# Attention and two gated layers on one core: the 1e-9 of the softmax on GpSimd, weight conversions once a pair and in two parts, and two transfers in another place

## The chip, the cores and the metric

The kernel runs on one core of one Trainium2 chip. Times are device microseconds of one execution. A core has TensorE (PE, matmuls and transposes), VectorE (DVE), ScalarE (ACT), GpSimd (POOL) and SyncE (SP), whose queue issues nearly all of this kernel's transfers. Each engine takes its instructions in a fixed order, and waits for semaphores of the others.

## What is computed

Causal attention with a decay, in float32, for 4 batches of 8 heads, 576 positions and 64 columns; its output, laid out as 2304 tokens of 512, runs through two gated layers.

```python
scores = np.matmul(q, k.transpose(0, 1, 3, 2)) / sqrt(D)
cum = np.cumsum(np.log(np.clip(f, 0.0001, 1.0)), axis=-1)
decay = cum[:, :, :, None] - cum[:, :, None, :]
scores = np.where(causal, -1e9, scores + decay)
attn = np.exp(scores - scores.max(-1, keepdims=True))
attn = attn / (attn.sum(-1, keepdims=True) + 1e-09)
x = np.matmul(attn, v)          # then (B * S, H * D)
x = (sigmoid(x @ w_gate) * (x @ w_val)) @ w_out
h = x @ w_in
return (h * np.clip(h + 3, 0, 6) / 6) @ w_out2
```

## The kernel before

**Pairs and steps.** Two heads make a pair; there are 16 pairs, and each is worked in four steps of query rows: first step s = 1 (the first 256 rows), second s = 2 and third s = 3 (128 rows each), fourth s = 4 (the 64 left over, both heads together). The loop near the end of the kernel counts steps by `t`, so pair i has t = 4i to 4i+3. Pairs 7 to 15 run their steps backwards. In step t TensorE multiplies the masks and the scores of unit t into PSUM (`st`); VectorE reads them, adds the decay and takes the least (`expo`, L500); ScalarE takes the exponential and sums it (L508). `norm` (L540 on) works one step later: VectorE adds 1e-9 to the sums (L543), takes the reciprocal (L544), and GpSimd multiplies the rows `e` by it (L546). Three steps after its scores a unit is turned by TensorE (`flip`, `tt<-ident,e`), and ScalarE copies it to `etA` or `etB`. So TensorE turns the fourth step of the pair before in the third step of this pair, behind that step's masks. In the third step also stand the products with v of the pair before (`values`, `pv`), whose result ScalarE and VectorE split in two (L645, L646) and SP stores in `x_d` (L650).

**Two banks.** The scores of a step take two of three PSUM tiles, so the masks of a step wait until VectorE has read the first tile of the step before. VectorE's reads thereby set TensorE's pace.

**Weights.** The weights of the gated layers come as float64 bits. A conversion (`single`, `convert`) takes a tile `raw` of 128x1024 words: VectorE shifts (L107) and merges (L108), ScalarE scales (L111), VectorE merges again (L114), and a high part (L64 on GpSimd, later L62 on ScalarE) and a low part (L65 on GpSimd) are made. `Converter.run` counts up a share per step and converts a tile when it comes to 1: before t = 24 it adds 0.38 (`CE`), then 0.65 (`CA`), near the end 0.12 (`CS`). That puts the first conversions at t = 6, 9, 11, 14, 17, 19 and 22. From t = 23 on TensorE also has a group of 12 products of the first gated layer in most steps (`fill.one`, `pg` and `pv` on `big`), which need the converted weights and `x_d` of the first four pairs (`big<-x_d`, L205).

**Order.** TensorE's order is written out by hand. For the other engines a scheduler chooses, among what `tc.issue_after` and `tc.high_priority` leave free. Pairs 7 on load q and k in blocks (`load_blocks`, 8 transfers of 72 KB a pair) and turn them with VectorE. The sums of logarithms, times -8, which these pairs need, are made in a tile `eight` of the pool that also holds the rows `e`, and stored from it (`cum_d<-eight`) at t = 2.

Of the kernel before, what the change touches and what calls it, by code (L numbers as in the profile page):

```python
# [7 lines left out]
F32 = mybir.dt.float32  # L8
# [12 lines left out]
def attn_moe_kernel(  # L21
# [18 lines left out]
    P = 128  # L40
# [62 lines left out]

    def single(a_, b_, raw, e_exp):
        low, high = raw[:, :, 0], raw[:, :, 1]
        with tc.issue_after(pace["dve"].ins) if pace["dve"] is not None else ExitStack():
            nc.vector.tensor_scalar(low, low, 29, None, ALU.logical_shift_right)  # L107
        nc.vector.scalar_tensor_tensor(low, high, -(2**31), low, ALU.bitwise_and, ALU.bitwise_or)  # L108
        e = high.bitcast(F32)
        if e_exp is nc.scalar:  # L110
            nc.scalar.activation(e, e, AF.Copy, scale=2.0**-112)  # L111
        else:
            e_exp.tensor_scalar(e, e, 2.0**-112, 1.0, ALU.mult, ALU.mult)
        nc.vector.scalar_tensor_tensor(low, high, 3, low, ALU.logical_shift_left, ALU.bitwise_or)  # L114
        return low.bitcast(F32).rearrange("p (a b) -> p a b", a=a_)

    def convert(dst_hi, dst_lo, raw, e_exp, e_hi, e_lo):
        a_, b_ = dst_hi.shape[1:]
        split_sbuf(dst_hi, dst_lo, single(a_, b_, raw, e_exp), e_hi, e_lo)

# [8 lines left out]
    class Half:  # L129
# [10 lines left out]
        def __call__(self, engs):  # L140
            self.load()
            t, ks = self.t, self.ks
            if not self.shape:
                a_, b_ = self.src.shape[1], self.src.shape[2] // 2
                t.append(single(a_, b_, self.raw, engs[0]))
# [3 lines left out]
            convert(t[0][:, 0, ks], t[0][:, 1, ks], self.raw, *engs)  # L149
            if ks.start > 0:  # L150
                t.append(True)

    class Converter:


        def __init__(self):
            self.jobs, self.due, self.ahead = [], 0.0, 0

# [15 lines left out]

        def run(self, n, engs):
            self.due += n
            if self.due >= 1.0:
                drain()
            while self.due >= 1.0 and self.jobs:
                self.due -= 1.0  # L180
                self.jobs.pop(0)(engs)
            for job in self.jobs[: self.ahead]:
                if isinstance(job, Half):
                    job.load()
            if not self.jobs:
                self.due = 0.0
# [14 lines left out]
    def load_x(src, c, kc):  # L201
        t0, T = chunks[c]
        x = xr[ring["x"] % len(xr)][:, :, :T]
        ring["x"] += 1
        nc.sync.dma_start(  # L205
            x.bitcast(F32), src[:, kc * P : (kc + 1) * P, t0 : t0 + T].rearrange("a p t -> p a t")
        )
        return x
# [80 lines left out]
    def cumulate():  # L289
# [12 lines left out]
        nc.sync.dma_start(cum_d[0], cum)  # L302
        return cum, pick

# [16 lines left out]
    class Pair:  # L321
# [17 lines left out]
        def load(self):  # L339

            new = lambda nm: nat.tile([P, NKT, 2, D], F32, tag="nat", name=nm)
            if self.blocks:
                self.qn, self.kn = (self.load_blocks(new(nm), src) for nm, src in (("qn", q), ("kn", k)))
                return
            self.qn = load_nat(new("qn"), q, self.b, self.hp, ())
            self.kn = load_nat(new("kn"), k, self.b, self.hp, ((0, k), (TAIL, q)))
# [193 lines left out]
        def norm(self, s):  # L540
            m, n = self.m[s], len(self.es[s])
            with behind(reads[-1]), tc.high_priority():
                nc.vector.tensor_scalar(m[:, 8 : 8 + n], m[:, 4 : 4 + n], 1.0e-9, None, ALU.add)  # L543
                pace["dve"] = nc.vector.reciprocal(m[:, 12 : 12 + n], m[:, 8 : 8 + n])  # L544
# [103 lines left out]
        def store(self):  # L648
            rows, cols = (slice(i * n, i * n + n) for i, n in ((self.hp, P), (self.b, S)))
            nc.sync.dma_start(x_d[:, rows, cols].rearrange("a p t -> p a t"), self.x.bitcast(F32))  # L650

# [590 lines left out]

    KD, KT, RT = 4, 7, 0

    CA, C0, CB, CC = 0.65, 4, (1.8, 1.0, 1.5, 1.7, 2.0), 1.0

    CE, CS = 0.38, 0.12

# [22 lines left out]
    warm_up(WU[0])  # L1271
    cum, pick = cumulate()
    pairs[0].load()
# [11 lines left out]
    def scores(t):  # L1285
# [5 lines left out]
        if i == 0 and nxt:  # L1291
            if p.i:
                nxt.load()
            nxt.load_decay()
            nxt.load_v()
        p.scores(s)
# [148 lines left out]
```

## Time and profile before

| | us |
|---|---|
| median of three runs | 1005.12 (1002.36 to 1005.62) |
| the profiled execution | 1003.57 |
| its span, first to last instruction | 1001.8 |
| TensorE busy | 986.5 |
| VectorE, ScalarE, GpSimd busy | 530.9, 476.9, 290.5 |

The page's busy shares are means over stages that differ: the attention takes the first 275 us or so, the two gated layers the rest. What bounds a stage is read from the busy times in stretches, from the waits, and from the instructions in order of time.

### The profile page before, as it was taken

The numbers are of one execution on the slowest core, as the hardware profiler recorded it, in microseconds if no ns is written. First come the engines' busy times: TensorE is split into PE (matmuls) and PEld (weight loads), VectorE is DVE, ScalarE is ACT, GpSimd is POOL, SyncE is SP. The second block draws the span as 40 slices with busy tenths as digits, with TensorE's granted clock in tenths as the row PEclk, the third lists the DMA queues.
The fourth block names the chain that finished last, engine by engine and source line by source line (L and its number), as shares of the span: only waits on it lengthen the run. The fifth ranks groups of instructions, "written<-read, shape, count | busy, mean of one in ns | idle before, by whom it ended". The sixth has DMA issues, their size and how long they took to land.

```text
span 1001.8 us, 16150 instructions
## 1 busy us (share of the span) xinstructions
PE 986.5 (98%) x5733; PEld 810.4 (81%) x5733; DVE 530.9 (53%) x1220; ACT 476.9 (48%) x1094; POOL 290.5 (29%) x360
## 2 busy tenths in 40 slices
PE   8889999999999999999999999999999999999998
PEld 4556766667688889988888888899899898998987
DVE  6777856645347543737777574553534443333322
ACT  6787677667634432424434343453444443433322
POOL 3675655545323220302334131111111111111110
PEclk9999999999999999999999999999999999999999
DMA  7999796744324352566977578654686845753211
GB/s 184 294 250 226 198 244 156 185 143 145 119 79 154 117 166 82 175 210 264 331 258 252 179 270 318 245 198 166 237 330 206 293 147 193 294 209 148 81 66 64
DMA packets 141072, 197.30 MB, mean 197 GB/s; under 512 B 84192, under 2 KB 93408, under 8 KB 136896
## 3 DMA queue, kind: packets, MB, share of 16 engines
q1 hardware_dynamic: 140944, 196.20, 59.9%
q8 instruction: 45, 0.74, 0.3%
q14 instruction: 35, 0.29, 0.1%
q10 hardware_dynamic: 48, 0.07, 0.0%
HBM read 142.88 MB, written 53.36 MB: 196 GB/s over the span
## 4 chain that ended last, share of the span: by engine, by line
PE 91%; DVE 3%; ACT 2%; DMA 2%; issue 1%; POOL 0%; SPq 0%; DVEq 0%; ACTq 0%; POOLq 0%
PE po L216 34%; PE pv L216 18%; PE u L216 17%; PE pg L216 15%; PE st L216 4%; PE tt L220 3%; DVE e L500 1%; DMA kn<-in_k_dram 1%; ACT e L508 1%; DMA cum_d<-eight 1%; DMA x_d<-x 0%; DVE raw L108 0%; ACT raw L111 0%; ACT etB L580 0%; PE o L216 0%
## 5 line engine op out<-in xcount | busy, mean ns | idle before, releaser
L216 PE MATMUL po<-w,big 128*128 128x512 f32 x864 | 200.5, 390 | 0.0
L216 PEld LDWEIGHTS po<-w,big 128*128 128x128 f32 x864 | 161.8, 188 | 32.8
L216 PE MATMUL pg<-big,wg 128*128 128x512 f32 (+1 forms) x720 | 161.9, 371 | 0.0
L216 PE MATMUL pv<-big,wv 128*128 128x512 f32 (+1 forms) x720 | 161.4, 371 | 0.0
L216 PE MATMUL po<-big,wo 128*128 128x512 f32 (+1 forms) x720 | 160.9, 371 | 0.2 <-DVE big L65 0.2
L216 PEld LDWEIGHTS pg<-big,wg 128*128 128x128 f32 x720 | 125.8, 189 | 27.2 <-issue 4.0
L216 PEld LDWEIGHTS pv<-big,wv 128*128 128x128 f32 x720 | 125.6, 189 | 26.8 <-issue 4.5
L216 PEld LDWEIGHTS po<-big,wo 128*128 128x128 f32 x720 | 125.6, 189 | 25.7 <-issue 2.2
L1160 DVE TENSOR_TENSOR h<-h,u 128x384 f32<-128x384 f32 x69 | 38.2, 554 | 154.0 <-PE u L216 154.0
L546 POOL TENSOR_SCALAR e<-e,m 128x256 f32<-128x256 f32 (+4 forms) x144 | 86.8, 617 | 48.8 <-DVE m L544 32.1
L508 ACT ACTIVATE e<-e,m 128x256 f32<-128x256 f32 (+4 forms) x144 | 83.6, 584 | 31.6 <-DVE m L500 20.3
L216 PE MATMUL u<-h,big 128*128 128x384 f32 x504 | 90.2, 336 | 0.4 <-DVE h L1160 0.4
L216 PE MATMUL u<-h,h 128*128 128x384 f32 x504 | 90.1, 336 | 0.0
L216 PEld LDWEIGHTS u<-h,big 128*128 128x128 f32 x504 | 88.3, 188 | 1.8 <-DVE h L1160 0.8
L216 PEld LDWEIGHTS u<-h,h 128*128 128x128 f32 x504 | 88.4, 188 | 1.0
L1109 POOL TENSOR_TENSOR big<-tail,big 128x384 fp32r<-128x384 f32 x30 | 30.5, 1018 | 196.5 <-PE u L216 115.5
L1157 ACT COPY h<-u 128x384 f32<-128x384 f32 x69 | 32.8, 475 | 111.5 <-PE u L216 111.5
L500 DVE CUSTOM_DVE_ANT_0 e<-st,dc 128x384 f32<-128x384 f32 (+3 forms) x110 | 53.5, 520 | 47.9 <-PE st L216 30.3
L872 DVE SCALAR_TENSOR_TENSOR sg<-sg,pv 128x512 f32<-128x512 f32 (+1 forms) x48 | 29.7, 618 | 92.3 <-PE pv L216 59.7
L111 ACT ACTIVATE raw<-raw 128x512 f32<-128x512 f32 x68 | 45.6, 682 | 67.1 <-DVE raw L108 64.5
L62 ACT CAST big<-sg 128x512 fp32r<-128x512 f32 (+1 forms) x60 | 34.8, 580 | 60.6 <-DVE sg L872 54.6
L114 DVE SCALAR_TENSOR_TENSOR raw<-raw 128x512 int32<-128x512 int32 x68 | 52.5, 782 | 19.4 <-ACT raw L111 18.9
(141 smaller groups left out, 1202.8 us busy)
## 6 DMA issues: line engine op xcount, KB each, us to landing
h<-xc_d SPq DMA_DIRECT2D x21, 768.0 KB, 7.2
big<-x_d SPq DMA_DIRECT2D x28, 512.0 KB, 5.8
raw<-in_moe_w_out_dram SPq DMA_DIRECT2D x28, 512.0 KB, 3.7
h<-wt_d SPq DMA_DIRECT2D x12, 1024.0 KB, 7.4
big<-wt_d SPq DMA_DIRECT2D x12, 1024.0 KB, 7.6
x_d<-x SPq DMA_DIRECT2D x16, 576.0 KB, 3.9
h<-wb_d SPq DMA_DIRECT2D x12, 768.0 KB, 4.6
big<-wb_d SPq DMA_DIRECT2D x12, 768.0 KB, 5.2
```

The costliest lines, as they stand in the source:

```text
L62: nc.scalar.copy(hi, src)
L111: nc.scalar.activation(e, e, AF.Copy, scale=2.0**-112)
L114: nc.vector.scalar_tensor_tensor(low, high, 3, low, ALU.logical_shift_left, ALU.bitwise_or)
L216: i = nc.tensor.matmul(*a, **k)
L220: i = nc.tensor.transpose(*a)
L500: i = nc.vector.tensor_tensor_reduce(out=e, in0=st, in1=d, op0=ALU.add, op1=ALU.min, scale=self.by, scalar=init, accum_out=m[:, a : a + 1],)
L508: nc.scalar.activation(e, e, AF.Exp, bias=m[:, a : a + 1], scale=-1.0, accum_out=m[:, 4 + b : 5 + b])
L546: pace["pool"] = nc.gpsimd.tensor_scalar(e, e, m[:, 12 + j : 13 + j], 1.0, ALU.mult, ALU.mult)
L872: pace["dve"] = nc.vector.scalar_tensor_tensor(sg, sg, 1.0, pv, ALU.add, ALU.mult)
L1109: (nc.vector if f else nc.gpsimd).tensor_tensor(lo, sg, hi.bitcast(F32), ALU.subtract)
L1157: nc.scalar.copy({0: u1, 2: u2, 3: p5}[s], o)
L1160: tt(c, c, o, ALU.add)
```

## The change

Five things are changed.

1. `norm`: the 1e-9 is added on GpSimd, with high priority, and only the reciprocal stays on VectorE behind the last read. 64 small instructions change engine.
2. `single` is cut in two. `begin_single` holds L107, L108 and L111; `end_single` the second merge (now L118), with the high and low part behind it. While `conv.parts` holds (t up to 22), the end is put off to the `conv.run` of the next step, and stands behind that step's last read of scores.
3. The shares `CA` and `CE` give way to a list of steps `CW`: one conversion at t = 6, 10, 14, 18 and 22 (in the third step of a pair, beside `values`), and then at 23, 24, 26 to 30.
4. `KD` goes from 4 to 5: the copy of k of pair 4 is on VectorE and not ScalarE, one half of that pair's `values` is in another PSUM pool, and the high parts are on GpSimd until t = 20 and not 16.
5. Transfers: `eight` is put in the tile `fl` of `cumulate` and not in one of the pool of `e`; pair 7's loads of q, and pair 6's of v, stand behind the store of pair 3's x, and pair 7's loads of k behind the load of that x for the first gated layer.

```diff
-    def single(a_, b_, raw, e_exp):
+    def begin_single(raw, e_exp):
         low, high = raw[:, :, 0], raw[:, :, 1]
...
-        nc.vector.scalar_tensor_tensor(low, high, 3, low, ALU.logical_shift_left, ALU.bitwise_or)
+
+    def end_single(a_, raw):
+        low, high = raw[:, :, 0], raw[:, :, 1]
+        with tc.issue_after(pace["dve"].ins) if conv.parts else ExitStack():
+            nc.vector.scalar_tensor_tensor(low, high, 3, low, ALU.logical_shift_left, ALU.bitwise_or)
         return low.bitcast(F32).rearrange("p (a b) -> p a b", a=a_)
...
         def __call__(self, engs):
             self.load()
+            begin_single(self.raw, engs[0])
+            if conv.parts:
+                conv.rest.append(lambda: self.end(engs))
+            else:
+                self.end(engs)
...
         def run(self, n, engs):
+            while self.rest:
+                self.rest.pop(0)()
             self.due += n
...
-                self.qn, self.kn = (self.load_blocks(new(nm), src) for nm, src in (("qn", q), ("kn", k)))
+                first = self.i == KT
+                with behind(pairs[NP - 1].stored if first else None):
+                    self.qn = self.load_blocks(new("qn"), q)
+                with behind(pace["x"] if first else None):
+                    self.kn = self.load_blocks(new("kn"), k)
                 return
...
             m, n = self.m[s], len(self.es[s])
+            with tc.high_priority():
+                nc.gpsimd.tensor_scalar(m[:, 8 : 8 + n], m[:, 4 : 4 + n], 1.0e-9, 1.0, ALU.add, ALU.mult)
             with behind(reads[-1]), tc.high_priority():
-                nc.vector.tensor_scalar(m[:, 8 : 8 + n], m[:, 4 : 4 + n], 1.0e-9, None, ALU.add)
                 pace["dve"] = nc.vector.reciprocal(m[:, 12 : 12 + n], m[:, 8 : 8 + n])
...
-    KD, KT, RT = 4, 7, 0
-
-    CA, C0, CB, CC = 0.65, 4, (1.8, 1.0, 1.5, 1.7, 2.0), 1.0
-
-    CE, CS = 0.38, 0.12
+    KD, KT, RT = 5, 7, 0
+
+    C0, CB, CS = 4, (1.8, 1.0, 1.5, 1.7, 2.0), 0.12
+
+    CW = (6, 10, 14, 18, 22, 23, 24, 26, 27, 28, 29, 30)
...
-            nxt.load_v()
+            with behind(pairs[NP - 1].stored if p.i == NP + 1 else None):
+                nxt.load_v()
...
-            eight = ep.tile([P, S], F32, tag="e", name="eight")[: B * H]
             nc.vector.tensor_scalar(eight, cum, -8.0, 1.0, ALU.mult, ALU.mult)
...
+        conv.parts = t <= CW[4]
         if t >= C0:
-            conv.run(CS if len(conv.jobs) <= 2 * NSA - 6 * NGA else CE if t < NQ * (KT - 1) else CA, EA if t < NQ * KD else EF)
+            conv.run(CS if len(conv.jobs) <= 2 * NSA - 6 * NGA else float(t in CW), EA if t < NQ * KD else EF)
```

TensorE's order is the same before and after, instruction for instruction. Three places where the others' order differs:

GpSimd, from the multiplication of the unit t = 10 (128x512) to that of t = 11 (128x576), before. `wv` is the weight that is converted there, `dt` the masked decay of the next pair:

```order
L546 TENSOR_SCALAR e<-e,m 128x512 x2
L386 AFFINE_SELECT dt<-dc 64x576 x2
L64 TENSOR_SCALAR wv_818<-raw 128x512
L546 TENSOR_SCALAR e<-e,m 128x576
L65 TENSOR_TENSOR wv_818<-raw,wv_818 128x512
```

The same stretch now (`wg` is the weight); those up to the units t = 7, 15 and 19 read alike:

```order
L560 TENSOR_SCALAR e<-e,m 128x512 x2
L399 AFFINE_SELECT dt<-dc 64x576 x2
L64 TENSOR_SCALAR wg_601<-raw 128x512
L556 TENSOR_SCALAR m<-m 128x1
L65 TENSOR_TENSOR wg_601<-raw,wg_601 128x512
L556 TENSOR_SCALAR m<-m 128x4
L560 TENSOR_SCALAR e<-e,m 128x576
```

Two additions have come in, and the low part of the weight (L65) stands ahead of the multiplication 128x576, not behind it.

VectorE in the third and fourth step of pair 1 (t = 6 and 7), before. `raw` is the tile being converted, `x` the split result, and the ISA rows are the reads of scores:

```order
L107 TENSOR_SCALAR raw<-raw 128x512
L646 TENSOR_TENSOR x<-pv,x 128x256
L108 SCALAR_TENSOR_TENSOR raw<-raw 128x512
L114 SCALAR_TENSOR_TENSOR raw<-raw 128x512
L646 TENSOR_TENSOR x<-pv,x 128x320
L500 ISA e,m<-st,dt 128x288
L500 ISA m 128x1
L500 ISA e,m<-st,dt,m 128x288
```

And now:

```order
L107 TENSOR_SCALAR raw<-raw 128x512
L660 TENSOR_TENSOR x<-pv,x 128x256
L108 SCALAR_TENSOR_TENSOR raw<-raw 128x512
L660 TENSOR_TENSOR x<-pv,x 128x320
L513 ISA e,m<-st,dt 128x288
L513 ISA m 128x1
L513 ISA e,m<-st,dt,m 128x288
L513 ISA m 128x1
L558 RECIPROCAL m<-m 128x2
L118 SCALAR_TENSOR_TENSOR raw<-raw 128x512
```

The second merge has moved behind both reads and the reciprocal, and the addition L543 is gone.

SP around the loads of pair 7's blocks (`32x18x32`) and the store of pair 3's x, before. The first row is the store of pair 2's x, the store in the last but two rows that of pair 3's:

```order
L650 DMA x_d<-x 128x2x576
L352 DMA qn<-in_q_dram 32x18x32 x2
L101 DMA raw<-in_moe_w_val_dram 128x2x512
L352 DMA qn<-in_q_dram 32x18x32 x2
L205 DMA big<-x_d 128x2x512
L352 DMA kn<-in_k_dram 32x18x32 x4
L365 DMA dc<-cum_d_89 128x1152
L311 DMA vn_151<-in_v_dram 128x4x64 x2
L315 DMA vn_151<-in_v_dram 64x2x64
L650 DMA x_d<-x 128x2x576
L101 DMA raw<-in_moe_w_val_dram 128x2x512
L352 DMA qn<-in_q_dram 32x18x32 x4
```

And now, again from the store of pair 2's x; the second store is that of pair 3's:

```order
L664 DMA x_d<-x 128x2x576
L214 DMA big<-x_d 128x2x512
L101 DMA raw<-in_moe_w_gate_dram 128x2x512
L378 DMA dc<-cum_d_89 128x1152
L664 DMA x_d<-x 128x2x576
L320 DMA vn_151<-in_v_dram 128x4x64 x2
L324 DMA vn_151<-in_v_dram 64x2x64
L365 DMA qn<-in_q_dram 32x18x32 x2
L214 DMA big<-x_d 128x2x512
L365 DMA qn<-in_q_dram 32x18x32 x2
L365 DMA kn<-in_k_dram 32x18x32 x4
```

Pair 7's eight loads now stand behind the store of pair 3's x, and its loads of k also behind the load `big` of that x.

## Rows read from the trace of the kernel before

**Rows 1.** Busy times in two stretches, one of each stage
```profile
core 0: us, PE busy (x) PEld busy (x) DVE busy (x) ACT busy (x) POOL busy (x), PEclk, DMA share, GB/s
50.00:75.00 25.00, 21.82 (x226) 13.27 (x226) 19.91 (x75) 21.65 (x67) 18.95 (x27) 1.00 0.94 251
...
300.00:325.00 25.00, 25.00 (x112) 20.67 (x112) 17.83 (x27) 11.75 (x19) 8.01 (x6) 1.00 0.50 152
```

**Rows 2.** TensorE's waits: us in total, times, longest us
```profile
PE st L216 <- DVE m L500: 3.9, 8, 2.1
PE st L216 <- ACT raw L111: 2.5, 2, 1.4
PE tt L220 <- POOL e L546: 1.4, 3, 0.6
```

**Rows 3.** TensorE in order of time: start, us, engine, line, operation, count [idle before]
```profile
32.02 0.51 PE L216 MATMUL st<-masks,identb 128*128 128x384 bf16 x2 [2.06 <-DVE m L500]
...
44.46 0.50 PE L216 MATMUL st<-masks,identb 128*128 128x384 bf16 x2
...
51.41 0.52 PE L220 MATMUL tt<-ident,e 64*128 64x64 f32 x10 [0.54 <-POOL e L546]
...
58.19 0.50 PE L216 MATMUL st<-masks,identb 128*128 128x384 bf16 x2 [0.70 <-DVE m L500]
...
63.88 0.53 PE L220 MATMUL tt<-ident,e 64*128 64x64 f32 x10
...
70.24 0.50 PE L216 MATMUL st<-masks,identb 128*128 128x384 bf16 x2 [0.20 <-DVE m L500]
...
82.98 2.99 PE L216 MATMUL pg<-big,wg 128*128 128x512 f32 x12
85.81 0.50 PE L216 MATMUL st<-masks,identb 128*128 128x384 bf16 x2
```

**Rows 4.** Busy times and granted clock in the 4 us behind the longest wait
```profile
32.00:36.00 4.00, 3.98 (x30) 2.67 (x32) 2.87 (x15) 2.40 (x7) 3.21 (x4) 0.57 1.11 239
```

**Rows 5.** VectorE in order of time, in third and fourth steps of pairs
```profile
27.46 0.69 DVE L500 CUSTOM_DVE_ANT_0 e<-st,dc 128x512 f32<-128x512 f32 x1 [1.30 <-DMA cum_d<-eight]
...
30.49 0.69 DVE L114 SCALAR_TENSOR_TENSOR raw<-raw 128x512 int32<-128x512 int32 x1 [0.73 <-ACT raw L111]
...
58.28 0.52 DVE L500 CUSTOM_DVE_ANT_0 e<-st,dt,m 128x288 f32<-128x288 f32 x1
...
71.32 0.17 DVE L544 RECIPROCAL m<-m 128x2 f32<-128x2 f32 x1
```

**Rows 6.** GpSimd in order of time, in the first and second steps of three pairs
```profile
49.97 0.67 POOL L64 TENSOR_SCALAR wv<-raw 128x512 fp32r<-128x512 f32 x1
50.60 0.75 POOL L546 TENSOR_SCALAR e<-e,m 128x576 f32<-128x576 f32 x1
51.32 1.30 POOL L65 TENSOR_TENSOR wv<-raw,wv 128x512 fp32r<-128x512 f32 x1
...
60.26 1.37 POOL L546 TENSOR_SCALAR e<-e,m 128x512 f32<-128x512 f32 x2 [0.78 <-ACT etB L580]
61.58 1.40 POOL L386 TENSOR_SCALAR_AFFINE_SELECT dt<-dc 64x576 f32<-64x576 f32 x2
...
71.66 1.81 POOL L546 TENSOR_SCALAR e<-e,m 128x512 f32<-128x512 f32 x2 [1.32 <-DVE m L544]
73.43 1.91 POOL L386 TENSOR_SCALAR_AFFINE_SELECT dt<-dc 64x576 f32<-64x576 f32 x2
```

**Rows 7.** Groups of GpSimd by form, first 275 us: busy us, mean ns | idle before
```profile
L546 POOL TENSOR_SCALAR e<-e,m 128x128 f32<-128x128 f32 x32 | 12.4, 388 | 21.3 <-DVE m L544 14.8 <-PE tt L220 4.5 <-ACT e L508 2.0
...
L546 POOL TENSOR_SCALAR e<-e,m 128x576 f32<-128x576 f32 x16 | 12.2, 761 | 1.2 <-ACT e L508 0.6 <-DVE m L544 0.3
```

**Rows 8.** DMA issues from 20 to 110 us: count, KB each, median us to landing
```profile
x_d<-x SPq DMA_DIRECT2D x6, 576.0 KB, 4.9
...
qn<-in_q_dram SPq DMA_DIRECT2D x16, 72.0 KB, 5.1
```

**Rows 9.** SP's queue in order of time: start, us, and what it issued
```profile
64.68 3.47 SPq L352 DMA_DIRECT2D kn<-in_k_dram  x4
```

More of the change, by code (lines that the diff above doesn't have):

```diff
@@ L113, in single @@
             e_exp.tensor_scalar(e, e, 2.0**-112, 1.0, ALU.mult, ALU.mult)
-        nc.vector.scalar_tensor_tensor(low, high, 3, low, ALU.logical_shift_left, ALU.bitwise_or)
+    def end_single(a_, raw):
+        low, high = raw[:, :, 0], raw[:, :, 1]
+        with tc.issue_after(pace["dve"].ins) if conv.parts else ExitStack():
+            nc.vector.scalar_tensor_tensor(low, high, 3, low, ALU.logical_shift_left, ALU.bitwise_or)
         return low.bitcast(F32).rearrange("p (a b) -> p a b", a=a_)
-    def convert(dst_hi, dst_lo, raw, e_exp, e_hi, e_lo):
-        a_, b_ = dst_hi.shape[1:]
-        split_sbuf(dst_hi, dst_lo, single(a_, b_, raw, e_exp), e_hi, e_lo)
     pace = {"dve": None, "pool": None}
@@ L141, in __call__, with end @@
             self.load()
+            begin_single(self.raw, engs[0])
[3 more added lines that the diff above has]
+                self.end(engs)
+        def end(self, engs):
             t, ks = self.t, self.ks
+            w = end_single(ks.stop - ks.start if ks else self.src.shape[1], self.raw)
             if not self.shape:
-                a_, b_ = self.src.shape[1], self.src.shape[2] // 2
-                t.append(single(a_, b_, self.raw, engs[0]))
+                t.append(w)
                 return
@@ L148, in __call__ @@
                 t.append(self.pool.tile(self.shape, F32R, tag=self.tag, name=self.nm))
-            convert(t[0][:, 0, ks], t[0][:, 1, ks], self.raw, *engs)
+            split_sbuf(t[0][:, 0, ks], t[0][:, 1, ks], w, *engs[1:])
             if ks.start > 0:
@@ L156, in __init__ @@
         def __init__(self):
-            self.jobs, self.due, self.ahead = [], 0.0, 0
+            self.jobs, self.due, self.ahead, self.rest, self.parts = [], 0.0, 0, [], False
         def cols(self, pool, tag, w, c0, nm):
@@ L204, in load_x @@
         ring["x"] += 1
-        nc.sync.dma_start(
+        pace["x"] = nc.sync.dma_start(
             x.bitcast(F32), src[:, kc * P : (kc + 1) * P, t0 : t0 + T].rearrange("a p t -> p a t")
@@ L302, in cumulate @@
         nc.sync.dma_start(cum_d[0], cum)
-        return cum, pick
+        return cum, pick, fl
     def behind(i):
@@ L649, in store @@
             rows, cols = (slice(i * n, i * n + n) for i, n in ((self.hp, P), (self.b, S)))
-            nc.sync.dma_start(x_d[:, rows, cols].rearrange("a p t -> p a t"), self.x.bitcast(F32))
+            self.stored = nc.sync.dma_start(x_d[:, rows, cols].rearrange("a p t -> p a t"), self.x.bitcast(F32))
     def mm3(o, wh, wl, xh, xl, first, last, free=False):
@@ L1271, in attn_moe_kernel @@
     warm_up(WU[0])
-    cum, pick = cumulate()
+    cum, pick, eight = cumulate()
     pairs[0].load()
```

## The prediction

> **What bounds the kernel now.** I read the busy times in stretches first: where the two gated layers run, TensorE is busy 25.00 of 25 us, and in the attention's early pairs 21.82 [rows 1]. TensorE's order and work are the same after the change, so it can win or lose only where TensorE waits. Second, TensorE's waits: nearly all lie before 100 us and add up to 7.8 us in three groups [rows 2]. Third, TensorE in order of time: I cut the early attention into cycles from one first-step mask to the next. They start at 32.02, 44.46, 58.19, 70.24 and 85.81 us, and the last holds one group of weight products of 2.83 us (82.98 to 85.81) [rows 3]. Without that group the four cycles take 12.44, 13.73, 12.05 and 12.74 us, 50.96 in all. These four, the wait ahead of them, and what follows until the products fill the waits are all that the change can move. In them VectorE, ScalarE and GpSimd are busy 19.91, 21.65 and 18.95 of 25 us [rows 1]: none has much to spare, and what counts is whose instruction TensorE stands behind.
>
> **Part one, ahead of the first cycle: gains.** The longest wait, 2.06 us, ends at 32.02, when VectorE has read the fourth step's scores [rows 3]. VectorE is late there for two reasons. It stood 1.30 us for the transfer `cum_d<-eight`, because that tile held a place in the pool of `e` [rows 5]. After the change `eight` is in another tile and its store stands far ahead, so this wait goes. And the second merge of the conversion, 0.69 us behind a wait of 0.73 for ScalarE, stood ahead of the read [rows 5]. It moves behind it; but the split of x, which stays ahead, waits for ScalarE behind the same scaling, so I take half of the merge, 0.3 us. Together -1.6 us; at most -2.06, which is the whole wait, and at least -1.0.
>
> What the wait also cost: in the 4 us behind it the granted clock is 0.57, on the way from the full 2.4 GHz down to 1.2 and back, that is 4 x 0.43 = 1.7 us [rows 4]. This is already inside the 12.44 of the first cycle, so it is counted below, with the cycles.
>
> **Part two, the four cycles: a new chain on GpSimd.** By the order, GpSimd works off between the fourth step's read and the turning of the fourth step's rows: two multiplications 128x512, two mask selects, the high part L64, an addition, the low part L65, another addition, and the multiplication 128x576. In before there is no addition, and L65 stands behind. I lay the new order out from rows, from the mask that starts a cycle:
>
> - VectorE's second read starts 0.09 later (58.28 against 58.19) and takes 0.52; from the reciprocal's start to the multiplication's is 0.34 (71.32 to 71.66) [rows 3, 5, 6]. The reciprocal now stands right behind the read, so the multiplications start at 0.95.
> - Two multiplications 128x512: 1.32 from their start to the next instruction's (60.26 to 61.58), or 1.77 (71.66 to 73.43). Two selects: 1.40 or 1.91 [rows 6].
> - L64 0.63 (49.97 to 50.60), L65 1.30, the multiplication 128x576 0.75, and 0.06 until TensorE turns (51.35 to 51.41) [rows 3, 6].
> - The additions on GpSimd are not in the trace. Between 128 and 576 columns the same operation takes 0.388 and 0.761 us [rows 7]: 0.00083 a column, which leaves 0.28 for a width of 1 to 4. The bounds are 0 (hidden in gaps) and 0.39 (the narrowest row). I take 0.28, twice: a small addition is nearest to the narrow row without its columns.
>
> With the shorter values the rows are ready at 0.95 + 1.32 + 1.40 + 0.63 + 0.28 + 1.30 + 0.28 + 0.75 + 0.06 = 6.97; with the longer ones at 7.93. The slow pair of rows ran beside a conversion on VectorE; now the merge of 0.69 runs beside the first multiplication for about half of it, so I take 0.35 on top of the short value: 7.3. In before TensorE came to this point at 5.69 in the third cycle (58.19 to 63.88), without a wait, and at 6.95 in the second (44.46 to 51.41), where L64 stood ahead and it waited 0.54 for GpSimd [rows 3]. So TensorE will wait here in every cycle, by 1.6 us against that third one. VectorE gives part of the wait to the mask ahead of it: its reciprocal of the fourth step now stands ahead of the second step's reads and waits for GpSimd's first addition, behind L64, at about 4.6.
>
> From this turning to the next cycle's mask took 6.36 us (63.88 to 70.24) and, with a merge ahead of the read, 6.78 (51.41 to 58.19) [rows 3]. With the merge moved I take 6.36. A cycle is then 7.3 + 6.36 = 13.66 us: the chain closes on itself, from read to read, so nothing in TensorE's order can shorten it. Four cycles 54.6 us against 50.96: **+3.7 us** (ends: 4 x 13.33, +2.4; 4 x 14.29, +6.2; with additions at nothing 4 x 0.56 = 2.2 less). The waits that leave, two of 2.5 us in sum for ScalarE's scaling [rows 2], are inside the old cycles.
>
> The Trainium skill, "SBUF — State Buffer", section "Who interferes with whom", says that a VectorE instruction with two SBUF inputs and a GpSimd instruction that reads SBUF exclude each other for a whole instruction. The merge is of that kind. By this rule the multiplication would lose up to the merge's whole 0.69 us and not 0.35: 4 x 0.34 = 1.4 us more. The trace has the slow multiplications at 1.77 against 1.32 [rows 6], which speaks for the smaller loss.
>
> **Part three, behind the cycles.** The third of GpSimd's waits, 0.6 us [rows 2], falls at t = 25, where L65 stood ahead of the multiplication 128x512. There the products give every step 2.83 us of cover [rows 3], and conversions stand differently: I take -0.6, and 0 as the other end. The catching up of conversions from t = 22 on has the same cover. The late loads of pair 7 are a rival, below. `KD` moves one copy of k and one high part a few us apart, under the chain above: nothing.
>
> **Sum.** -1.6 + 3.7 - 0.6 = **+1.5 us**, from about -1.5 to +5 with not all ends at once. Against the profiled execution of 1003.57 (span 1001.8 and 1.8 around it) this is 1005.1. The median of the runs shown, 1005.12, lies 1.55 above that execution; I put the forecast at half of that, 1005.9. A measurement of this kernel tells about 0.3%, 3 us, from no change: the forecast is no difference that can be told, on the slow side.
>
> **Rivals.**
>
> *GpSimd is not the limit.* If its chain overlaps better than laid out, the four cycles run like the best of before, 12.05 us [rows 3], which is 48.2 against 50.96. Then -1.6 - 2.8 - 0.6 = -5.0 us: 998.6 by the profiled execution, faster. For it: the waits for ScalarE and for merges do leave, and VectorE gives up 64 additions. Against it: it needs 5.7 us where rows add up to 7.0 or more, and in the second cycle L64 alone was enough to make TensorE wait.
>
> *The clock falls in the cycles: slower.* Behind the 2.06 us wait the clock fell and cost 1.7 us [rows 3, 4]; behind shorter waits, such as those of 1.4 [rows 2], the table of stretches shows 1.00 [rows 1]. The chain gives each cycle waits of about 1.6 us at two neighbouring places, between the two. If they act as the long one did, each fall costs 1.7: with two of the four cycles +1.5 + 3.4 = +4.9, 1008.5; with all four 1011.9. [...] The Trainium skill, "TensorE: Matmul & The Clock Gate", section "What's actually happening", says that the slow clock is the default and activity lifts it, which the 0.57 agrees with.
>
> *Pair 7's q and k come late.* Their loads now stand behind the store of pair 3's x, which lands 4.9 us after its issue; then come the load of that x, two of q, four of k (3.47 us of issue) and 5.1 to land [rows 8, 9]: about 15.5 us. VectorE turns k between the two reads of the fourth step one cycle later, some 14 us after that store. It would stand 1.5 us, mostly under the product group of 2.83 us; if the store takes longer, 2 us come through: +3.5, 1007.1.
>
> **How the numbers follow.** The forecast has 0.52 (0.03 faster by over 0.3%, 0.37 within, 0.12 slower), GpSimd not the limit 0.20 (faster), the clock 0.18 (0.16 slower), late loads 0.10 (0.04 slower, 0.06 within). That makes 0.23 faster, 0.45 within 0.3%, 0.32 slower. The range reaches down to 999, the upper half of the first rival with the offset of half the 1.55 in it, and up to 1010, two falls of the clock with the same offset and the forecast's own upper end.
>
> **What would show it.** Right: in the profile after, cycles of 13 to 14.3 us between first-step masks; TensorE waits at the turning of the fourth step's rows for GpSimd's multiplication 128x576, and at the mask ahead of it for VectorE; the additions at 0.2 to 0.4 us each; the wait ahead of 32 us down to 0.5. Wrong: no wait for `e` from GpSimd in the third steps, cycles near 12, or additions that take a different time by much; waits of TensorE behind 100 us that before had not; the clock below 1.00 in stretches behind 40 us.

## Result and the profile after

The changed kernel takes 1018.37 us in the median of five runs (1014.45 to 1018.7), the kernel before 1003.02 beside it: a ratio of 1.0142, with an interval of 1.0121 to 1.0164. It is slower by 15.4 us, about ten times what the forecast of +1.5 us said. The profiled execution took 1018.70 us, its span is 1016.9.

To see where the time goes I cut both traces at the same instructions of TensorE: the first product of a pair with its values (`pv<-etA`, t = 6, 10, 14 and so on), numbered 1 to 16. All runs below are read by this table (us; the last column is the median of the timed runs). The stretches come from the one profiled execution of each run, which isn't always near that median: e15's took 1000.19 us against 1002.87, e3's 1006.84. e3's median counts one slow execution of 1090.37 us, without which it is 1005.20; the ratios leave it out.

| kernel | start of values 1 | 1 to 5 | 5 to 6 | 7 to 8 | 11 to 12 and 15 to 16 | time |
|---|---|---|---|---|---|---|
| before | 25.24 | 52.78 | 22.16 | 19.91 | 17.26, 17.52 | 1003.02 |
| after | 26.72 | 58.77 | 26.90 | 21.82 | 17.68, 17.74 | 1018.37 |
| e1, additions on VectorE | 26.81 | 49.82 | 25.40 | 21.85 | 18.86, 18.87 | 1009.49 |
| e2, loads not held | 25.05 | 57.77 | 22.36 | 21.91 | 17.68, 17.74 | 1012.52 |
| e3, before, additions on GpSimd | 25.18 | 52.10 | 25.60 | 19.73 | 17.16, 17.53 | 1005.44 |
| e4, e1 and e2 together | 25.20 | 49.71 | 28.91 | 21.82 | 18.82, 18.58 | 1011.4 |
| e5, before, `eight` moved | 25.27 | 50.75 | 22.42 | 19.88 | 17.25, 17.53 | 1001.59 |
| e6, dc of pair 7 first | 24.96 | 61.15 | 23.02 | 21.85 | 17.62, 17.71 | 1015.2 |
| e7, e1 with the old steps | 25.79 | 53.03 | 20.79 | 19.88 | 17.89, 18.61 | 1004.74 |
| e8, conversions not cut | 25.03 | 49.81 | 27.34 | 21.82 | 17.62, 17.72 | 1008.65 |
| e9, e1 and e6 together | 25.14 | 49.70 | 27.72 | 21.86 | 18.79, 18.90 | 1009.28 |
| e10, e1 with another list | 25.92 | 51.99 | 20.78 | 19.51 | 17.89, 18.89 | 1003.52 |
| e11, that list, not cut | 25.76 | 53.83 | 20.83 | 19.75 | 17.63, 17.75 | 1004.12 |
| e12, e10, share from 0.15 | 25.80 | 51.96 | 22.37 | 19.50 | 17.26, 17.52 | 1002.15 |
| e13, one conversion at t = 4 | 30.43 | 49.10 | 22.74 | 19.47 | 17.19, 17.53 | 1005.34 |
| e14, six by t = 22, one at 4 | 30.75 | 49.36 | 23.56 | 19.48 | 17.24, 17.53 | 1006.66 |
| e15, evenly spread | 25.85 | 48.61 | 22.32 | 19.90 | 17.26, 17.52 | 1002.87 |
| e16, e15, q not held | 25.43 | 48.56 | 27.51 | 19.91 | 17.25, 17.53 | 1005.2 |

After minus before, at the values of pair 16 (289.94 against 275.13): 14.81 us. Of it 1.5 is there before the first cycle, 6.0 comes in the four cycles (1 to 5), 4.7 between the fifth and sixth values, 1.9 between the seventh and eighth, 0.6 in two places behind 200 us. The gated layers behind take the same time (727.0 and 726.7 us).

TensorE's waits, which answer to [rows 2], were 7.8 us in three groups and are 14.4 in the two that the forecast named (us in total, times, longest):

```profile
PE st L225 <- DVE m L513: 7.3, 8, 2.2
PE tt L229 <- POOL e L560: 7.1, 6, 1.5
PE pv L225 <- ACT etB L594: 1.4, 1, 1.4
```

The third row is a new wait, at 132.06, between the seventh and eighth values.

The busy times in stretches (columns as in [rows 1]) show the clock falling in two of three stretches, and the transfers' share between 50 and 75 us down to 0.73 from 0.94:

```profile
50.00:75.00 25.00, 19.98 (x174) 11.38 (x173) 13.60 (x47) 16.40 (x51) 16.11 (x31) 0.86 0.73 218
75.00:100.00 25.00, 21.36 (x194) 13.87 (x190) 15.16 (x56) 18.09 (x54) 13.56 (x23) 1.00 0.90 208
100.00:125.00 25.00, 21.81 (x144) 15.19 (x144) 18.05 (x43) 15.10 (x35) 15.54 (x23) 0.93 0.79 202
```

**A cycle.** TensorE in order of time, which answers to [rows 3]: one undisturbed cycle from 32.05 to 46.22, 14.17 us, and two products of the next:

```profile
32.05 0.50 PE L225 MATMUL st<-masks,identb 128*128 128x384 bf16 x2 [0.62 <-DVE m L513]
...
37.67 0.29 PE L225 MATMUL st<-masks,identb 128*128 128x128 bf16 x2 [0.93 <-DVE m L513]
39.50 0.52 PE L229 MATMUL tt<-ident,e 64*128 64x64 f32 x10 [1.54 <-POOL e L560]
...
46.22 0.50 PE L225 MATMUL st<-masks,identb 128*128 128x384 bf16 x2 [0.64 <-DVE m L513]
...
55.02 1.44 PE L225 MATMUL pv<-etA,vn 128*64 128x256 f32 x8
56.24 3.39 PE L225 MATMUL pv<-etB,vn 128*64 128x320 f32 x20
```

The wait for GpSimd's `e` is the same 1.54 us in all four cycles, and the wait for VectorE ahead of it 0.91 to 0.93: the two places that the forecast named. Behind the second of these waits the products take 1.44 and 3.39 us instead of 0.87 and 2.22, because the clock has fallen (granted 0.68 from 56 to 60 us); behind the third it falls too. GpSimd in the same cycle is the chain of the forecast, row for row:

```profile
32.91 1.65 POOL L560 TENSOR_SCALAR e<-e,m 128x512 f32<-128x512 f32 x2 [2.77 <-PE tt L229]
34.51 1.39 POOL L399 TENSOR_SCALAR_AFFINE_SELECT dt<-dc 64x576 f32<-64x576 f32 x2
35.99 0.68 POOL L64 TENSOR_SCALAR wg<-raw 128x512 fp32r<-128x512 f32 x1
36.76 0.19 POOL L556 TENSOR_SCALAR m<-m 128x1 f32<-128x1 f32 x1
37.03 1.30 POOL L65 TENSOR_TENSOR wg<-raw,wg 128x512 fp32r<-128x512 f32 x1
38.41 0.19 POOL L556 TENSOR_SCALAR m<-m 128x4 f32<-128x4 f32 x1
38.70 2.35 POOL L560 TENSOR_SCALAR e<-e,m 128x576 f32<-128x576 f32 x5
```

The last row groups five multiplications; the first is the one of 128x576, and TensorE turns its rows at 39.50. From the mask at 32.05 that is 7.45 us; the forecast had 7.3.

**Behind the cycles.** The step that the forecast took for covered is t = 24 to 26. SP's queue in order of time:

```profile
86.93 2.83 SPq L365 DMA_DIRECT2D qn<-in_q_dram  x4
89.85 2.32 SPq L365 DMA_DIRECT2D kn<-in_k_dram  x4
92.28 0.44 SPq L378 DMA_DIRECT2D dc<-cum_d  x1
```

GpSimd there:

```profile
97.19 0.41 POOL L462 TENSOR_SCALAR_AFFINE_SELECT dz<-dc 128x256 f32<-128x256 f32 x1 [4.58 <-DMA dc<-cum_d]
97.58 1.36 POOL L560 TENSOR_SCALAR e<-e,m 128x512 f32<-128x512 f32 x2
...
100.38 0.19 POOL L556 TENSOR_SCALAR m<-m 128x1 f32<-128x1 f32 x1
```

VectorE:

```profile
100.60 0.17 DVE L558 RECIPROCAL m<-m 128x1 f32<-128x1 f32 x1 [3.75 <-POOL m L556]
100.68 1.57 DVE L107 TENSOR_SCALAR raw<-raw 128x512 int32<-128x512 int32 x1
...
104.12 0.69 DVE L118 SCALAR_TENSOR_TENSOR raw<-raw 128x512 int32<-128x512 int32 x1 [0.72 <-ACT raw L111]
104.73 0.55 DVE L513 CUSTOM_DVE_ANT_0 e<-st,dc 128x384 f32<-128x384 f32 x1
```

TensorE:

```profile
105.34 0.28 PE L225 MATMUL st<-masks,identb 128*128 128x128 bf16 x2 [2.21 <-DVE m L513]
106.61 0.80 PE L229 MATMUL tt<-ident,e 64*128 64x64 f32 x10 [0.99 <-ACT etB L594]
107.18 2.05 PE L225 MATMUL st<-kp,qp 64*128 64x512 f32 x4
```

The decay `dc` of pair 7 is issued at 92.28, behind the blocks of pair 8 (before: 82.28, behind those blocks too). Of these 10 us, 7.5 are there at the fifth values already. It is issued 6.8 us after those values; before the change that was 4.3, in e6 and e2 it is 1.4 and 1.5. GpSimd's select `dz` stands 4.58 us for it, ahead of the multiplication 128x512 and of an addition; VectorE's reciprocal stands 3.75 us for that addition; behind the reciprocal stand a whole conversion (L107 to L118) and only then the reads of the scores; TensorE waits 2.21 and 0.99 us, and its clock falls once more (2.05 us for scores that take 1.08 at full clock).

GpSimd's wait for the decay is not new. GpSimd and VectorE at the same place before the change:

```profile
87.99 0.41 POOL L449 TENSOR_SCALAR_AFFINE_SELECT dz<-dc 128x256 f32<-128x256 f32 x1 [6.09 <-DVE m L500]
88.97 0.16 DVE L544 RECIPROCAL m<-m 128x1 f32<-128x1 f32 x1
```

The wait of 6.09 us is put down to VectorE, but the decay, issued at 82.28, took 5.7 us to land, which is the moment at which `dz` starts. In e3 and e5, with the transfers in the same order, the trace names the decay for waits of 6.01 and 6.41. Before, it cost TensorE at most the 0.64 us behind it: VectorE made its own addition, and its reciprocal waited for nothing on GpSimd.

### The profile page after: what moved, and what is told of

Its sections match the earlier page's. It is cut to its first block, busy times and chain, and to the rows that moved or that the text cites. A ratio compares the mean times of both kernels' runs of the same rounds, so it can differ in the third digit from the quotient of the medians.

```text
span 1016.9 us, 16113 instructions
## 1 busy us (share of the span) xinstructions
PE 991.9 (98%) x5733; PEld 811.5 (80%) x5733; DVE 519.9 (51%) x1157; ACT 477.5 (47%) x1093; POOL 298.6 (29%) x424
## 4 chain that ended last, share of the span: by engine, by line
PE 90%; DVE 3%; POOL 3%; issue 2%; ACT 1%; DMA 1%; SPq 0%; POOLq 0%; ACTq 0%; DVEq 0%
PE po L225 33%; PE u L225 17%; PE pv L225 17%; PE pg L225 15%; PE st L225 5%; PE tt L229 3%; DVE e L513 1%; POOL e L560 1%; POOL dt L399 1%; DMA kn<-in_k_dram 1%; DVE raw L108 0%; PE o L225 0%; ACT e L521 0%; DVE x L660 0%; POOL m L556 0%
## 5 line engine op out<-in xcount | busy, mean ns | idle before, releaser
L560 POOL TENSOR_SCALAR e<-e,m 128x256 f32<-128x256 f32 (+4 forms) x144 | 82.4, 586 | 48.1 <-DVE m L558 30.6
L111 ACT ACTIVATE raw<-raw 128x512 f32<-128x512 f32 x68 | 45.2, 676 | 73.4 <-DVE raw L108 70.0
L118 DVE SCALAR_TENSOR_TENSOR raw<-raw 128x512 int32<-128x512 int32 x68 | 51.2, 763 | 19.0 <-ACT raw L111 18.5
```

Of the source, the lines that this page charges most:

```text
L560: pace["pool"] = nc.gpsimd.tensor_scalar(e, e, m[:, 12 + j : 13 + j], 1.0, ALU.mult, ALU.mult)
```

## Experiments

The theory after the result: (a) the cycles are long since L65 stands between GpSimd's multiplications; (b) behind them the loss comes from transfers and conversions that the change put off. The rivals: the additions by themselves, or the cut of the conversions.

**Undoing one part each (e1, e2, e3, e4).** e1 is the changed kernel with the addition on VectorE:

```diff
-            with tc.high_priority():
-                nc.gpsimd.tensor_scalar(m[:, 8 : 8 + n], m[:, 4 : 4 + n], 1.0e-9, 1.0, ALU.add, ALU.mult)
             with behind(reads[-1]), tc.high_priority():
+                nc.vector.tensor_scalar(m[:, 8 : 8 + n], m[:, 4 : 4 + n], 1.0e-9, None, ALU.add)
```

> The changed kernel with the 1e-9 added on VectorE again; all else as changed. GpSimd's order then has L65 behind the multiplication 128x576 again. Theory A (the additions, and the L65 that they let ahead of 128x576, made the four cycles long): the cycles fall from 14.2, 15.2, 15.3 and 13.3 us to about 12 to 12.5, TensorE's waits of 0.91 and 1.54 us in each go, and with them the falls of the clock; the waits near 100 us (2.2 and 1.0) stay, since the loads are still late: about 1007 to 1010 us. Theory B (one conversion a pair with its end behind the fourth step's reads is itself what blocks GpSimd): the cycles stay above 13 and the time near 1015. Theory C (nearly all comes from the moved loads): above 1013.

Measured: 1009.49 us, ratio 1.0062 (1.0042 to 1.0082). The cycles take 12.45 us each. GpSimd in the first one:

```profile
33.37 1.63 POOL L559 TENSOR_SCALAR e<-e,m 128x512 f32<-128x512 f32 x2 [2.96 <-DVE m L557]
34.95 1.39 POOL L399 TENSOR_SCALAR_AFFINE_SELECT dt<-dc 64x576 f32<-64x576 f32 x2
36.44 0.68 POOL L64 TENSOR_SCALAR wg<-raw 128x512 fp32r<-128x512 f32 x1
37.06 0.78 POOL L559 TENSOR_SCALAR e<-e,m 128x576 f32<-128x576 f32 x1
37.77 1.33 POOL L65 TENSOR_TENSOR wg<-raw,wg 128x512 fp32r<-128x512 f32 x1
```

The cycles are theory A's. With the additions gone the scheduler also puts L65 behind the multiplication 128x576, so e1 takes away two things at once. The waits of 2.2 and 1.0 us near 100 us, which theory A left standing, are gone too; that 5 to 6 still takes 25.40 goes with another one: VectorE stands 3.72 us for pair 7's q, and the first product group 2.08 for VectorE.

e2 keeps the additions and holds no load: `behind(...)` around pair 7's q and k and pair 6's v becomes `behind(None)`.

> The changed kernel with the three loads (q, k of pair 7, v of pair 6) free to be issued as before; the additions stay on GpSimd. Theory A: the four cycles stay at 13.3 to 15.3 us, with the waits of 0.91 and 1.54; GpSimd's wait of 4.6 us for the decay of pair 7 goes, and with it TensorE's waits of 2.2 and 1.0 near 100 us: 1011 to 1014 us. Theory C: the cycles get shorter too, below 1008. If the loads have no part in it: 1018.

Measured: 1012.52 us, ratio 1.0099 (1.0079 to 1.0119). From the fifth values to the sixth it is 22.36 us instead of 26.90: the three holds cost 4.5 us there, in this arrangement. The cycles stay long, as theory A had it: three of four are 14.2 us.

e3 is the kernel before with the additions on GpSimd, the diff of e1 turned round.

> The kernel before with nothing but the 1e-9 on GpSimd. Its order keeps L65 behind or far ahead of 128x576. Theory A (what costs is mainly the L65 that stands ahead, 1.30 us, and the additions at 0.2 to 0.3 each): 0.3 to 0.6 us a cycle, 1004 to 1006 us. If the additions cost by themselves what was seen in the cycles: 1008 or more.

Measured: 1005.44 us, ratio 1.0022 (1.001 to 1.0033). The time is theory A's, the place is not. In the old arrangement the additions cost the cycles nothing (52.10 against 52.78). From 5 to 6 they cost 3.4 us, with no load held: the select `dz` stands 6.01 us for the decay, about as long as before, but now an addition stands behind it, and VectorE's reciprocal behind that:

```profile
92.11 0.16 DVE L545 RECIPROCAL m<-m 128x1 f32<-128x1 f32 x1 [4.45 <-POOL m L543]
```

TensorE's waits there are 1.05 and 0.98 us, the kind that the changed kernel has with 2.21 and 0.99.

e4 undoes both.

> The changed kernel with both undone: additions on VectorE, loads free; what is left is the split conversion once a pair, the tile of the sums, and KD 5. Theory A: cycles of about 12 us, the wait ahead of the first cycle down from 2.06 to about 0.6, none of the waits near 100 us: 997 to 1001 us, faster than before. Theory B: not faster than before, 1003 or more.

Measured: 1011.4 us, ratio 1.0089 (1.0069 to 1.0108): theory B, and 10 us off theory A. The parts don't add up. With fast cycles and no holds TensorE waits 2.69 us for the load `big` of pair 3's x and 3.35 for `e`, and 5 to 6 takes 28.91 us.

**`eight` alone (e5).** The kernel before with the sums in `fl`.

> The kernel before, with one edit: the sums times -8 are made in the tile of the cumulated logarithms and not in one of the pool of e. Theory A (the forecast's part one: the 2.06 us wait ahead of the first cycle is that tile's): the first values of a pair start at 24.0 to 24.3 us and not at 25.24, the clock falls no more between 25 and 50 us, and the time is 1000 to 1002 us against 1002.6. Theory B (in this stage the transfers set the end, and what the engines win early they wait for later): the first values come earlier too, but the fifth pair's values to the sixth's take 1 to 2.5 us longer than 22.16, and the time is 1002 to 1004.

Measured: 1001.59 us against 1002.2, ratio 0.9998 (0.9986 to 1.001). Theory A's mark was wrong: the first values lie ahead of the wait. Its mechanism is there: the wait is 0.69 instead of 2.06, the clock stays at 1.00 from 25 to 50 us, and the span is 1.8 us shorter. The medians don't show it.

**The decay first (e6).** In the changed kernel pair 8's blocks now stand behind pair 7's decay:

```diff
-            return nc.sync.dma_start(self.dc.rearrange(...), both.to_broadcast([P, 2 * S]))
+            self.sent = nc.sync.dma_start(self.dc.rearrange(...), both.to_broadcast([P, 2 * S]))
...
-                with behind(pairs[NP - 1].stored if first else None):
+                ahead = pairs[KT].sent if self.i == KT + 1 else None
+                with behind(pairs[NP - 1].stored if first else ahead):
```

> The changed kernel, with one edit: the block loads of q and k of pair 8 stand behind the load of pair 7's decay (dc) on SP. Theory A (in t = 24 to 26 GpSimd stood 4.58 us for that decay, which was queued behind pair 8's blocks, and TensorE and VectorE behind it): from the fifth pair's values to the sixth's it takes 22 to 23.5 us and not 26.90; the cycles ahead stay as they are; time 1013 to 1015.5 against the changed kernel's 1018.4. Theory B (the weight conversions that were put off to t = 22 to 24 cost that time): 25.5 to 27 us there, time 1017 to 1019.

Measured: 1015.2 us, ratio 1.012 (1.01 to 1.014). 5 to 6 takes 23.02 instead of 26.90, as theory A had it. The late decay makes up 3.9 of the 4.7 us that are lost there, in the changed kernel. (1 to 5 is 61.15, since the clock fell in more of the cycles: 0.80 from 50 to 75 us.)

**The conversions at the old steps (e7).** e1 with

```diff
-    CW = (6, 10, 14, 18, 22, 23, 24, 26, 27, 28, 29, 30)
+    CW = (6, 9, 11, 14, 17, 19, 22, 24, 26, 27, 29, 30)
-        conv.parts = t <= CW[4]
+        conv.parts = t <= CW[6]
```

> The changed kernel with the 1e-9 added on VectorE again, and its conversions at the steps of the kernel before (6, 9, 11, 14, 17, 19, 22, 24, 26, 27, 29, 30), still cut in two up to t = 22. Theory A (putting five conversions off and catching up by t = 30 costs what the version with the additions on VectorE still loses behind the cycles): from the seventh pair's values to the eighth's 19.9 us and not 21.85, from the fifth's to the sixth's 22 to 24 and not 25.40; time 1004 to 1006.5 against 1009.5. Theory B (the transfers cost it, not the conversions): the two stretches stay at 25 and 21.8; time 1008 to 1011.

Measured: 1004.74 us, ratio 1.0015 (1.0003 to 1.0027). 7 to 8 is back at 19.88, and 5 to 6 at 20.79 without any wait of TensorE. In GpSimd's order `dz` has come behind the multiplication 128x512 and finds its decay there:

```profile
87.06 1.36 POOL L559 TENSOR_SCALAR e<-e,m 128x512 f32<-128x512 f32 x2 [0.91 <-PE tt L229]
88.37 1.39 POOL L399 TENSOR_SCALAR_AFFINE_SELECT dt<-dc 64x576 f32<-64x576 f32 x2
89.84 0.46 POOL L462 TENSOR_SCALAR_AFFINE_SELECT dz<-dc 128x256 f32<-128x256 f32 x1
```

The transfers' share from 50 to 75 us is 0.91 again, and the loads of the weights stand earlier. So the list of steps costs 1.9 us at 7 to 8, and more at 5 to 6. There the run moves the conversions and the place of `dz` together, and doesn't tell the two apart. In the cycles the list gains: at the old steps they take 53.03 against e1's 49.82, with two waits of 1.63 us for ScalarE's scaling, the kind of [rows 2].

**Not cut (e8).** The changed kernel with `conv.parts = False`, the additions on GpSimd.

> The changed kernel with its conversions not cut in two: the second merge and what follows stand in the same step again. The additions stay on GpSimd. GpSimd then has L64 and L65 ahead of the two multiplications 128x512 and nothing but an addition ahead of the one of 128x576. Theory A (the cycles are long because L65 stands between the multiplications; the additions alone cost next to nothing): the first pair's values to the fifth's take 50.5 to 54 us and not 58.77, time 1009.5 to 1014. Theory B (the additions' own time and their waits on GpSimd make the cycles long): 56 to 59 us, time 1016 to 1019.

Measured: 1008.65 us, ratio 1.0064 (1.0049 to 1.0079). First to fifth values: 49.81 us, the same as e1, with all additions on GpSimd:

```profile
29.94 0.66 POOL L64 TENSOR_SCALAR wg<-raw 128x512 fp32r<-128x512 f32 x1 [1.47 <-DVE raw L118]
30.68 1.30 POOL L65 TENSOR_TENSOR wg<-raw,wg 128x512 fp32r<-128x512 f32 x1
31.96 1.37 POOL L560 TENSOR_SCALAR e<-e,m 128x512 f32<-128x512 f32 x2
33.27 1.39 POOL L399 TENSOR_SCALAR_AFFINE_SELECT dt<-dc 64x576 f32<-64x576 f32 x2
34.76 0.19 POOL L556 TENSOR_SCALAR m<-m 128x1 f32<-128x1 f32 x1
35.31 0.75 POOL L560 TENSOR_SCALAR e<-e,m 128x576 f32<-128x576 f32 x1 [0.36 <-DVE m L558]
```

L64 and L65 lie ahead of the multiplications, in GpSimd's idle time. With e1 this settles (a), for this list of steps: neither the additions (e8) nor the cut (e1) by themselves make the cycles long, but the two together do. Only then does L65 stand between the multiplications. No run moves L65 alone; by the rows of the changed kernel it takes 1.38 us there and the two additions 0.56 with their gaps, against 1.72 between the cycles (14.17 and 12.45). The loss at 5 to 6 stays (27.34).

**e1 with the decay first (e9).**

> The changed kernel with the 1e-9 added on VectorE again and pair 8's block loads behind the load of pair 7's decay (dc). Theory A (behind the cycles the decay that comes late is the larger loss): from the fifth pair's values to the sixth's 22 to 23.5 us and not 25.40, the four cycles still 49.8, time 1006 to 1008 against 1009.5 with the additions alone undone. Theory B (the conversions that are caught up there cost it): 24.5 to 25.5 us there, time 1009 to 1010.5.

Measured: 1009.28 us, ratio 1.0059 (1.004 to 1.0079), 5 to 6 at 27.72: neither theory. With fast cycles another transfer is late. VectorE in order of time:

```profile
82.05 0.71 DVE L412 STREAM_TRANSPOSE qp<-qn 128x512 f32<-128x512 f32 x1 [5.60 <-DMA qn<-in_q_dram]
```

TensorE behind it:

```profile
83.52 5.49 PE L225 MATMUL pg<-big,wg 128*128 128x512 f32 x12 [3.96 <-DVE x L660]
```

VectorE stands 5.60 us for pair 7's q, which is held behind the store of pair 3's x, and the first product group takes 5.49 us at the lower clock instead of 2.99. This is the forecast's third rival; it showed only in runs whose cycles are faster than those of the change.

**Other lists (e10 to e14).** e10 is e1 with `CW = (6, 9, 10, 14, 17, 18, 22, 24, 26, 27, 29, 30)` and the cut up to t = 22.

> The changed kernel with the 1e-9 added on VectorE again, and conversions at 6, 9, 10, 14, 17, 18, 22, 24, 26, 27, 29, 30: seven by t = 22 as in the kernel before, but all in second and third steps of pairs up to there, where the run with the steps of before showed no wait for the scaling. Theory A (what the change loses is the place of L65, the conversions put off and the decay): first values to the fifth's 49.8 to 50.8 us, fifth to sixth 20.5 to 22.5, seventh to eighth 19.9; time 1000.5 to 1003.5. Theory B (with faster cycles the transfers are late): fifth to sixth 24 us or more, time 1004 to 1007.

Measured: 1003.52 us, ratio 1.0007 (0.9997 to 1.0017). 5 to 6 and 7 to 8 as in theory A; but 1 to 5 is 51.99, above it, since two conversions in neighbouring steps make two first-step masks wait 1.51 and 1.54 us for VectorE. e11 has that list, not cut, with the additions on GpSimd.

> The changed kernel, its additions on GpSimd, with the conversions not cut in two and at the steps 6, 9, 10, 14, 17, 18, 22, 24, 26, 27, 29, 30. GpSimd's L64 and L65 then stand ahead of the multiplications 128x512, never between them and the one of 128x576. Theory A (the additions are free where L65 is not in the chain): first values to the fifth's 49.8 to 51.5 us, fifth to sixth 20.5 to 23, time 1001 to 1004. Theory B (two conversions close together, at t = 9 and 10 and at 17 and 18, stretch the chain on GpSimd): 52 to 54 us in the cycles, time 1004 to 1008.

Measured: 1004.12 us, ratio 1.0009 (0.9998 to 1.0019); the cycles are theory B's, 53.83 us. e12 is e10 with the running share of the conversions starting at 0.15 and not 0.

> As the run before last with the list 6, 9, 10, 14, 17, 18, 22, 24, 26, 27, 29, 30 and the additions on VectorE, and one edit more: the running share of the conversions starts at 0.15, the remainder that the kernel before has at t = 30, so that the later conversions fall at t = 38, 46, 54 again. Theory A (the step at which the later conversions fall costs the loss behind 200 us): the stretches that took 17.89 and 18.89 us there take 17.26 and 17.5 again, time 1001 to 1002 (2 us less). Theory B (the order of the engines there has other reasons): they stay, time 1003 to 1004.

Measured: 1002.15 us, ratio 0.9996 (0.9988 to 1.0005). The two stretches behind 200 us are back at 17.26 and 17.52. The old shares leave 0.15 at t = 30, the list leaves 0, so the later conversions came a step later. e13 is e12 with conversions at 4, 6, 9, 13, 17, 20, 22, 24, 26, 27, 29, 30.

> As the run with the remainder of 0.15, but with conversions at 4, 6, 9, 13, 17, 20, 22, 24, 26, 27, 29, 30: no two in neighbouring steps up to t = 22. Theory A (it is neighbouring conversions that cost the cycles 1.1 us each): the first pair's values to the fifth's 49.8 to 51 us and not 52, fifth to sixth 20.5 to 22, time 999 to 1001. Theory B (a conversion in a fourth or first step costs a wait for the scaling whatever its neighbours): 51.5 to 53.5 us, time 1001 to 1004.

Measured: 1005.34 us, ratio 1.0028 (1.0014 to 1.0041). The cycles are short (49.10), but the conversion at t = 4 costs 4.6 us at the start, with a wait of 3.61 us for VectorE.

e14 is e12 with six conversions by t = 22, at 4, 6, 9, 14, 17 and 22, and the next at 23. It was expected at 49.8 to 50.3 us in the cycles, 20.5 to 22.5 from 5 to 6 and 999 to 1001 us in all, or, if the one load put off was enough to make transfers late, at 23 to 26 and 1002 to 1005. Measured: 1006.66 us, ratio 1.0047 (1.0032 to 1.0062). The cycles are short (49.36) and 5 to 6 takes 23.56, the second theory's stretch; the time is longer than either had it, since the conversion at t = 4 costs 5 us at the start again.

**Evenly spread, and q not held (e15, e16).** e15 is e13 with 23 in place of 4.

> As the run with the remainder of 0.15 and the additions on VectorE, but with conversions at 6, 9, 13, 17, 20, 22, 23, 24, 26, 27, 29, 30. Theory A (the run with one at t = 4 lost at the start only, and its cycles were short because no two conversions are neighbours): first values at 25.2 to 25.9 us, from there to the fifth's 49 to 50.5, fifth to sixth 22 to 23.5, time 999 to 1001. Theory B (the transfers set the end, so that the sixth pair's values come at 101 to 103 us however fast the cycles are): fifth to sixth 25 to 28 us, time 1003 to 1006.

Measured: 1002.87 us (1000.04 to 1006.46), ratio 1.0002 (0.9991 to 1.0013). The profiled execution took 1000.19 us and shows the stretches of theory A or better; but it is the second fastest of twelve, and the median doesn't follow. e16 takes away the hold on q.

> As the run before it, with pair 7's loads of q not held behind the store of pair 3's x. Theory A (the hold makes q late by more than it brings for x): the wait of VectorE for q goes, and the time is 0.5 to 2 us less than the run before it. Theory B (the transfers as a whole are late, and another one takes q's place): another transfer's wait comes up (the load of x, the decay), and the time is the same within 1 us or more.

Measured: 1005.2 us, ratio 1.0031 (1.0019 to 1.0043), theory B. The wait for q is gone, and the decay's is there. GpSimd in order of time:

```profile
88.21 0.41 POOL L462 TENSOR_SCALAR_AFFINE_SELECT dz<-dc 128x256 f32<-128x256 f32 x1 [9.49 <-DMA dc<-cum_d]
```

TensorE behind it:

```profile
90.60 0.46 PE L229 MATMUL tt<-ident,e 64*128 64x64 f32 x8 [3.92 <-POOL e L559]
```

The hold on q, one of the three that together cost 4.5 us in the changed kernel (e2), gains 2.3 us here. No version is measurably faster than the kernel before.

## The prediction, point by point

- **Part one, -1.6: right.** From the first-step mask of the pair before to the first cycle's it is 11.82 us after (20.23 to 32.05) and 13.33 before (18.69 to 32.02): -1.51, and in e5 alone -1.38. But in this execution the clock fell behind 11 us (granted 0.50 from 11 to 14 us) and gave 1.5 us back. e6, with the same code up to there, has the earlier mask at 18.48 and no fall, so the edit doesn't bring it about in every execution.
- **Part two, +3.7: mechanism and places right, the size too small (+7.0).** The undisturbed cycle is 14.17 us instead of 13.66: 0.15 more in the chain, and 0.36 at the next mask, where VectorE is 0.64 late. The two additions take 0.19 us each, where I had 0.28, but each has a gap of 0.08 to 0.10 about it. The two multiplications beside the merge took 1.60 to the next instruction (32.91 to 34.51), 0.28 above the short value, where I had 0.35. The four cycles took 14.17, 15.18, 15.30 and 13.27 us, the last without its closing wait, under the product group: +6.96 against before. Of the 3.3 us that are missing, the two falls of the clock are 2.1 (15.18 and 15.30 against 14.17), the longer cycle the rest.
- **Rival two, the clock: it came, in two of four cycles, as its smaller case had it.** Each of these cycles is 1.0 or 1.1 us longer, where I had 1.7. The waits ahead are the same in all four, 0.91 to 0.93 and 1.54 us. e2 has the same waits, and a granted clock of 1.00 from 50 to 75 us, where the changed kernel has 0.86, but 0.93 from 25 to 50, where that has 1.00. What decides between equal waits stays open.
- **Part three, -0.6: the step that failed.** It gave +7.8 us (14.81 less 6.99 at the fifth cycle's mask). It rested on "the products give every step 2.83 us of cover", and that cover did not hold for an engine that stands 4.6 us for a transfer with its successors in line behind it. Two things were left out. I had priced the additions in the cycles alone, and put nothing down for those of t = 24 to 26, which stand behind `dz`; the trace of before had GpSimd standing 6.09 us there, right ahead of the L65 to which I put the 0.6 us down. The additions alone bring 3.4 us (e3). And I had read SP's order and asked who waits for pair 7's q and k; I did not ask what else was queued behind them on SP. It was the decay of pair 7, which made `dz` later still (e6: -3.9 us with it ahead; e2: -4.5 with the loads free). The catching up of conversions, which I also took for covered, cost 1.9 us more at 7 to 8 (e7), and the remainder of the share about 0.6 (e12, seen there at 2 us). These make 6.4 of the 7.8 us; the rest has no run of its own, nor has `KD`, which I took at nothing.
- **Rival three, q and k late:** not in the changed kernel, whose cycles are slower; in e1 and e9, with cycles of 12.4 us, VectorE stood 3.7 and 5.6 us for q.
- **Rival one, GpSimd not the limit:** wrong for the change; its price, cycles of 12.05, is near what e1 and e8 reach (12.45).

## What to carry to other kernels

When a change alters what an engine with a fixed order does, price the order, not the added instructions: two additions of 0.19 us, with the 1.3 us operation that came in front along with them, made cycles of 14.17 us out of e1's 12.45. Do it at every place where the instructions stand: what waits at no cost today costs as soon as something urgent is put behind it, as the additions were behind `dz`. When a load is held back, list everything behind it on its queue, and for each who waits for it and what stands behind that one. Parts of such a change don't add up (e1 and e2 gave -8.9 and -5.9, together -7.0), so the best of each stretch is not the best kernel.

## What was not expected of the hardware

- GpSimd's addition on 128x1 to 128x4 takes 0.19 us, half of the 0.388 of 128 columns; where VectorE runs the merge L108 beside it, it takes 0.50 and 0.51 (at 88.43 and 102.94 us in the changed kernel).
- VectorE's shift L107 took 1.57 us at 100.68, while GpSimd ran L65 (100.64 to 101.96), and 0.41 to 0.43 in the six conversions ahead of it; it took 1.25 at 128.67, beside another L65 (128.32 to 129.63).
- The same waits bring the clock down in one cycle and not in the next, and executions of one program spread over 6 us (e15). A stretch of a single trace shows where time goes, but the falls of that one execution are in it: the same cycles take 58.77 us in the changed kernel's trace and 61.15 in e6's.
